# A recurrent attention block and a hashed mixture of experts in one kernel: which queue some loads stand on, where the inversion's steps stand on VectorE, and routing products cut into quarters

## The chip, the cores and the metric

The kernel runs on one core of a Trainium2 chip. The metric is the device time of one execution in microseconds (us); lower is better. Engines are called as in the profile: PE is TensorE's matmuls, PEld its weight loads, DVE is VectorE, ACT is ScalarE, POOL is GpSimd, SP is SyncE. A "q" behind an engine (SPq, POOLq) means the queue on which that engine issues DMAs.

## The reference, cut to what matters

```python
# attention: B, H, S, D = 4, 8, 768, 40, float32; state is D x D for each (batch, head)
for t in range(S):
    y[:, :, t] = einsum('bhd,bhde->bhe', r[t], state)
    Sa = einsum('bhde,bhe->bhd', state, a[t])
    state = state * w[t] - outer(Sa, b[t]) + outer(v[t], k[t])
x = y.transpose(0, 2, 1, 3).reshape(B * S, H * D)          # 3072 x 320
# experts: 8 of them, w1 320 x 1024, w2 1024 x 320
expert = token_ids * 2654435761 % 8
for e in range(8):
    out[expert == e] = relu(x[expert == e] @ w1[e]) @ w2[e]
```

## The kernel before

**Attention.** The sequence is cut into chunks of 64 steps. A tile is one chunk of two batches with all heads; there are 24 tiles, `u` = 0 to 23. Inside a chunk the recurrence becomes a triangular system: the products of the chunk's vectors are formed on PE (`z_ps`, `t_ps`, `a_ps`), the triangular matrix is inverted, and the state is carried from tile to tile by a chain of small products. The inversion (`group_i`) is done on DVE for four tiles at a time: one transposition (`nb`, L585), then 31 steps of two instructions each (`outer`, L595, and `ub`, L598), then transpositions out (`ut`, L603, and `um`, L609). The rest of a tile's chain is in `tile_m` and `tile_b`: `x_ps` and `u_ps` apply the inverse, `c_ps`, `rc_ps`, `nc_ps`, `s_ps`, `sd_ps`, `r_ps` and `y_ps` follow. DVE masks `rc_ps` into `mr` (L743), updates the state `sc` (L770) and forms `xs`, the product of y's PSUM tile with the decay `py` (L787), which POOL or SP stores to `x_rows` in DRAM. `decays` prepares the cumulative decays of `w` for each round of four tiles, on POOL and DVE.

**Order by ticks.** Nothing in this part is ordered by a scheduler. Each piece is registered with `at_tick(tick, ...)`, all pieces are sorted by tick, and every engine runs its instructions strictly in that order. Tile `u` runs its chain in tick `u + 8`; the 15 steps of a chain (`STEPS`) stand at fifteenths of a tick, so `rcv`, with DVE's `mr`, is at 4/15, `a` at 7/15 and `y` at 13/15. Group `gi` of the inversion starts at tick 4·gi + 3.5. Equal ticks are ordered by `order`, then by registration.

**PSUM.** `psum(...)` hands out two double-bank tiles in turn (`psa`), `bank(...)` two single banks in turn (`psb`). A product in a tile waits until what was two requests earlier in that ring has been read out. `x_ps` of a tile with `ti` not 0 stands at tick 0.1, right behind `y_ps` and `u_ps`, and takes the bank of `y_ps`, which `xs` reads.

**Routing** (`routing`, a generator whose pieces are advanced at the ticks of `when`) loads the token ids (`tok`), forms a one-hot `mine`, its sums by PE (`sums_ps`), ranks and slots on DVE, and in the end `slots_ps`: 24 products of a one-hot 128x128 (`at_pos`) with 53 columns (`tiles_f`), four at a time in six places between tiles 19 and 21. Its result gives the row indices of gather and scatter.

**Loads.** `first_weights` loads the first expert's weights in 12 DMAs, at ticks 20.5 to 27.1; each is `paced`, that is, it waits for the PE instruction that stands last before it. SP's queue also carries the tiles' inputs.

**Experts.** Behind the ticks a scheduler orders each engine's instructions at compile time, by program order and its own estimates; at run time each engine runs in the order fixed then. For each expert: `gather` (POOL, indirect DMAs), transposition on PE, `xt`; `up` (L1035, L1039; relu into `ht` on DVE for odd `f` and on ACT for even `f`, L1042 and L1044); `down` (L1059); a scatter (POOL, L1049). Expert 1's weights wait for expert 0's last gather; later ones for free buffers. Beside it the kernel reads all of `w` again, in 24 loads of 160 KB (`look`, tile `wt`, four buffers), and DVE checks that no value had to be clamped (`judge`, L1086 and L1087); only if one had does a slow loop run at the end. The first 16 of these loads stand on POOL's queue, the last 8 on SP's.

Of the kernel before, what the change touches and what calls it, by code (L numbers as in the profile page):

```python
# [8 lines left out]
F32 = mybir.dt.float32  # L9
I32 = mybir.dt.int32  # L10
AF = mybir.ActivationFunctionType
OP = mybir.AluOpType
# [6 lines left out]
def kernel(  # L19
# [13 lines left out]
    nc = tc.nc  # L33
    B, H, S, D = r.shape
    N, DM = out.shape
    E, _, F = moe_w1.shape
    assert (B * S, H * D) == (N, DM)
    P = 128
    C = 64
# [3 lines left out]
    NU = NCH * NG  # L43
    BLK = 32
    GRP = 4
    TPP = N // P
# [9 lines left out]
    NT = NST + NOV  # L56
    STEP = 8

    def pool(name, bufs, **kw):
        return ctx.enter_context(tc.tile_pool(name=name, bufs=bufs, **kw))  # L60

    const = pool("const", 1)
    route = pool("route", 1)
# [47 lines left out]
    def apool(name, bufs, **kw):  # L111
        return a_ctx.enter_context(tc.tile_pool(name=name, bufs=bufs, **kw))
# [7 lines left out]
    def turn_of(i):  # L120
        taken[i] += 1
        return taken[i] % 2
    psu = apool("psu", 1, space=bass.MemoryType.PSUM)

    R = 2 * C
    LAG = 8
# [23 lines left out]
    def at_tick(tick, step=None, order=0):  # L150
        if step is not None:
            tick += STEPS.index(step) / len(STEPS)

        def add(f):
            plan.append((round(tick, 4), order, len(plan), f))
            return f
        return add
# [52 lines left out]
    def psum(name):  # L210
        return psa.tile([P, 2, 512], F32, tag=f"psa{turn_of(0)}", name=name)

    def bank(shape, name):
        n = 1
        for s in shape[1:]:
            n *= s
        t = psb.tile([P, 512], F32, tag=f"psb{turn_of(1)}", name=name)[:, 0:n]
        return t if len(shape) == 2 else t.rearrange("p (x y) -> p x y", x=shape[1])

    def half(i):  # L220
        return slice(i * C, (i + 1) * C)
# [4 lines left out]
    def quarters():  # L226

        for hp in range(HP):
            for p in range(2):
                for be in range(2):  # L230
                    yield hp, p, be
# [3 lines left out]
    def mm(out_, lhsT, rhs, start=True, stop=True):  # L235
        pe_last[0] = nc.tensor.matmul(out_, lhsT=lhsT, rhs=rhs, start=start, stop=stop, skip_group_check=True).ins  # L236
# [383 lines left out]
    def tile_m(u, t0):  # L620

        x = tiles[u]
        gi, ti = divmod(u, GRP)

        t_x = t0 - 1.9 if ti else t0 - 1.4

        @at_tick(t_x)
        def _():
            ut = groups[gi]["ut"]
            x["x_ps"] = p = bank([P, H, BLK], "x_ps")  # L630
            for hp, par, be in quarters():
                h = hx(par, hp)
                top, low = slice(be * C, be * C + BLK), slice(be * C + BLK, (be + 1) * C)
                mm(p[low, h, :], x["no"][top, par, hp, BLK:], ut[top, ti * H + h, :])

        @at_tick(t_x + 0.115 if ti else t_x)
        def _():
            p = x.pop("x_ps")
            x["xi"] = xi = xi_r(u)
            for be in range(2):  # L640
                low = slice(be * C + BLK, (be + 1) * C)
                nc.scalar.copy(xi[low], p[low])

        @at_tick(*((t0 - 0.62,) if u and ti == 0 else (t0 - 1, "u")))
        def _():
            um, xi = groups[gi]["um"], x["xi"]
            x["um"] = um[:, ti * H:(ti + 1) * H, :]
            p = bank([P, H, BLK], "u_ps")
            for hp, par, be in quarters():
                h = hx(par, hp)  # L650
                top, low = slice(be * C, be * C + BLK), slice(be * C + BLK, (be + 1) * C)
                mm(p[top, h, :], xi[low, h, :], um[low, ti * H + h, BLK:])
            for be in range(2):
                top = slice(be * C, be * C + BLK)
                nc.scalar.copy(um[top, ti * H:(ti + 1) * H, BLK:], p[top])
# [147 lines left out]
    t_a = STEPS.index("a") / len(STEPS)  # L803
    decays(0, -9.0, -8.0, (-7.9, -7.6), -7.7, -7.5, -7.49, -7.48, None, -6.9, -7.2, -7.1)
    decays(1, -8.5, -7.09, (-7.08, -7.0), 0.85, 1.01, 1.02, 1.2, 1.03, 3.6, 1.05, (2.85, 2.0))
    decays(2, -5.5, 3.45, (5.61, 5.9), 6.2, 6.555, 6.56, 6.57, 6.561, 8.22, 6.58, (7.62, 7.55))
    for ri in range(3, NR):
        t = ri * RN * NG
        decays(ri, t - 5.8, *((7.75, (8.3, 8.9), 8.95) if ri == 3 else (t - 5.2, (t - 5.1, t - 3.9), t - 3.55)), t - 2.6, t - 2.59, t - 2.5, t - 2.45, t - 1.88, t - 2.4, (t - 0.9, t - 1.48))
# [5 lines left out]
    for gi in range(NU // GRP):  # L815
        t0 = gi * GRP + GRP - 1 + t_a
        if gi == 0:
            group_i(gi, 3.43, 3.47, 6.4, 6.401)
        else:
            group_i(gi, t0 + 0.03, t0 + 0.06, t0 + 2.68, gi * GRP + LAG - 0.99)  # L820


    ovin = route.tile([P, E], F32)
# [5 lines left out]
    def routing():  # L829
# [27 lines left out]
                                     op0=OP.mult, op1=OP.add)  # L857
# [56 lines left out]
        tiles_f = work.tile([P, (HC + 1) * D], F32, tag="qb", name="tiles_f", bufs=1)[:, 0:TPP * NT].rearrange("p (c n) -> p c n", n=NT)  # L914
# [5 lines left out]
        for i in range(3):  # L920
            shape, tag = ([P, BLK, BLK], "nb") if i == 1 else ([P, BH * D], "pt")
            at = work.tile(shape, F32, tag=tag, name="at_pos", bufs=1)[:]
            at = (at.rearrange("p a b -> p (a b)") if i == 1 else at[:, 0:per * P]).rearrange("p (c n) -> p c n", n=P)
            nc.vector.tensor_tensor(at, col[:].unsqueeze(1).to_broadcast([P, per, P]),
                                    place[:, 1, i * per:(i + 1) * per].unsqueeze(2).to_broadcast([P, per, P]), op=OP.is_equal)
            yield
            if i == 0:
                full_ps = psu.tile([P, BLK, BLK], F32, tag="ub", name="slots_ps")[:].rearrange("p s t -> p (s t)")[:, 0:NT]
            for c in range(per):
                k = i * per + c  # L930
                mm(full_ps, at[:, c], tiles_f[:, k], start=k == 0, stop=k == TPP - 1)
                if c % 4 == 3:
                    yield
        full = route.tile([P, NT], I32)
        nc.vector.tensor_scalar(full[:], full_ps, float(N), None, op0=OP.add)
        nc.vector.tensor_copy(idx_all[:, 0:NMT], full[:, 0:NMT])
        nc.sync.dma_start(slot_dram[:].rearrange("(p c) -> p c", p=P), full[:])
        for q in range(4):
# [18 lines left out]


    steps = routing()
    when = [22.25 + 0.1 * i for i in range(10)] + [24.4, 26.55, 26.9, 27.35, 27.75, 27.9, 28.35, 28.75, 28.9, 29.35, 29.75, 29.9, 29.95, 30.5]  # L960
    for t in when:
        at_tick(t, order=7)(lambda: next(steps, None))

# [2 lines left out]
    def first_weights():  # L966
        w1, w2 = moe_w1[0], moe_w2[0]
        h = HC * D
        a = [carry.tile([P, h], F32, tag="pb", name=f"w1_0{i}") for i in range(2)]
        b = carry.tile([P, 2, h], F32, tag="qt", name="w2_0", bufs=1)  # L970

        def hi(f):
            return a[f // 4][(f % 2) * C:(f % 2 + 1) * C, F + (f // 2 % 2) * P:F + (f // 2 % 2 + 1) * P]
        first_w[1] = lambda f, c: a[c][:, f * P:(f + 1) * P] if c < 2 else hi(f)
        first_w[2] = lambda f: b[:, f // 4, (f % 4) * DM:(f % 4 + 1) * DM]
        for i in range(2):
            for j in range(2):
                cols = slice(j * F // 2, (j + 1) * F // 2)
                yield nc.sync.dma_start(a[i][:, cols], w1[i * P:(i + 1) * P, cols])
            for x in range(2):  # L980
                yield nc.sync.dma_start(a[i][x * C:(x + 1) * C, F:].rearrange("p (f i) -> p f i", i=P),
                                        w1[2 * P:DM].rearrange("p (f x i) -> p x f i", x=2, i=P)[:, x, 2 * i:2 * i + 2])
        for i in range(2):
            for j in range(2):
                c0 = 4 * i + 2 * j
                yield nc.sync.dma_start(b[:, i, 2 * j * DM:2 * (j + 1) * DM].rearrange("p (c d) -> p c d", d=DM),
                                        w2[c0 * P:(c0 + 2) * P].rearrange("(c p) d -> p c d", p=P))

    weights = first_weights()
# [82 lines left out]
    wq = w.rearrange("b h (q t) e -> (b h q) (t e)", q=P // BH)  # L1072
    m = S * D * BH // (P * WP)
    seen = []

    def look(n):
        for i in range(len(seen), len(seen) + n):
            wt = mwork.tile([P, m], F32, tag="wt", name="wt", bufs=n)
            (nc.gpsimd if i < 16 else nc.sync).dma_start(wt[:], wq[:, i * m:(i + 1) * m])  # L1079
            seen.append(wt)  # L1080

    def judge(n):
# [61 lines left out]
    sel = seq.tile([P, B * H], F32, name="selq")  # L1144
# [5 lines left out]
    full = [P, DQ, D]  # L1150

    some = nc.values_load(ctl_i[0:1, 3:4], min_val=0, max_val=1)  # L1152
    with tc.For_i(0, some, 1):
        nblk = nc.values_load(ctl_i[0:1, 0:1], min_val=0, max_val=S // STEP)
        with tc.For_i(0, nblk, 1) as i:
            tsl = bass.ds(i * STEP, STEP)
            vec = {}
            for nm, src in (("w", w), ("a", a), ("b", b), ("k", k)):
                t = vec[nm] = seq.tile([P, STEP, D], F32, tag=f"in_{nm}", name=f"in_{nm}")
# [3 lines left out]
            for nm, src in (("v", v), ("r", r)):  # L1163
                t = vec[nm] = seq.tile([P, STEP, DQ], F32, tag=f"in_{nm}", name=f"in_{nm}")
# [34 lines left out]
        start = nc.values_load(ctl_i[0:1, 1:2], min_val=0, max_val=NST)  # L1199
        end = nc.values_load(ctl_i[0:1, 2:3], min_val=NST, max_val=NT)  # L1200
        with tc.For_i(start, end, 1) as i:
# [9 lines left out]
            w1 = load_w1(moe_w1[bass.ds(ereg, 1)].rearrange("one d f -> (one d) f"), "w1_ov")  # L1211
# [38 lines left out]
```

## Time and profile before

| | us |
|---|---|
| median of 3 runs (lowest to highest) | 698.65 (697.24 to 699.78) |
| the profiled execution | 697.15 |
| its span, first to last instruction | 695.4 |

| stretch of the span, us | PE busy | DVE busy | granted PE clock |
|---|---|---|---|
| 0 to 95 (loads, decays, first inversions) | 44.69 | 78.94 | 0.80 |
| 95 to 150 | 50.32 | 44.45 | 0.93 |
| 150 to 209 | 56.20 | 43.84 | 0.96 |
| 209 to 268 | 56.12 | 43.24 | 0.96 |
| 268 to 330 (routing begins) | 55.12 | 43.21 | 0.97 |
| 330 to 380 | 46.40 | 32.79 | 0.94 |
| 380 to 418 (last tiles) | 33.48 | 10.97 | 1.00 |
| 418 to 460 (experts begin) | 25.61 | 17.62 | 0.72 |
| 460 to 695 (experts) | 223.86 | 36.88 | 0.99 |

A row of a timeline is: start in us, duration in us, engine, line, operation, tile written and tiles read, shape, and xN for N instructions drawn together; in brackets stands how long the engine was idle just before and whose result ended the wait. PE's float32 product is recorded as two matmuls, so "x32" is 16 products. A granted clock of 1.00 is TensorE's upper level (2.4 GHz), 0.50 its lower one (1.2 GHz).

### The profile page before, as it was taken

Reading aid. Unit: us, or ns where it says so; the run is one execution under the profiler, and the core shown is the slowest. Engines: PE = TensorE matmul, PEld = TensorE weight load, DVE = VectorE, ACT = ScalarE, POOL = GpSimd, SP = SyncE. Lnnn points to the kernel's source line nnn. Section 1 sums busy time; section 2 is a strip of 40 time slices with the busy share of each in tenths; the row PEclk is TensorE's granted clock in tenths of the full one; section 3 lists DMA queues with packets and bytes.
Section 4 is the critical chain, followed back from the end, with each engine's and each line's share of the span. In section 5 each row is a group of like instructions: output and inputs, shape, how many; then the busy total and the mean of one; then the engine's idle time right before and its main releaser. Section 6 shows DMA issues by size and latency. Waiting matters only on the chain. (4 is left out here: it accounts for less than half of the span.)

```text
span 695.4 us, 23888 instructions
## 1 busy us (share of the span) xinstructions
PE 591.8 (85%) x10418; PEld 439.5 (63%) x10418; DVE 351.9 (51%) x747; ACT 263.8 (38%) x524; POOL 260.3 (37%) x352
## 2 busy tenths in 40 slices
PE   0356679989989999978899984699999999999995
PEld 0245668878878887867788872265655556565654
DVE  6969898677677857756873223335111111111110
ACT  1568547656666675646345320111011111111110
POOL 4439579785575733521131016312203030210101
PEclk9978569999999999999899995799999999999998
DMA  9875056655655455722333215992322442120000
GB/s 137 150 115 122 3 116 131 145 114 118 130 117 126 101 112 113 158 54 62 83 90 84 51 43 172 328 330 77 111 83 69 152 143 86 47 94 19 29 4 30
DMA packets 158125, 73.83 MB, mean 106 GB/s; under 512 B 132222, under 2 KB 151231, under 8 KB 158016
## 3 DMA queue, kind: packets, MB, share of 16 engines
q1 hardware_dynamic: 147840, 52.92, 34.3%
q0 software_dynamic: 5824, 18.36, 8.9%
q10 hardware_dynamic: 4352, 0.98, 1.2%
q8 instruction: 83, 1.36, 0.8%
q14 instruction: 26, 0.21, 0.1%
HBM read 56.71 MB, written 12.15 MB: 99 GB/s over the span
## 5 line engine op out<-in xcount | busy, mean ns | idle before, releaser
L1059 PE MATMUL dn_ps<-w,ht 128*128 128x320 f32 x384 | 105.1, 433 | 0.0
L1039 PE MATMUL up_ps<-xt,w 128*128 128x416 f32 x256 | 94.9, 524 | 0.0
L1059 PEld LDWEIGHTS dn_ps<-w,ht 128*128 128x128 f32 x384 | 72.7, 190 | 32.4 <-issue 2.4
L1049 POOL DMA_INDIRECT out_dram<-o,idx_all x26 | 26.1, 1002 | 171.4 <-ACT o L1048 167.3
L1039 PEld LDWEIGHTS up_ps<-xt,w 128*128 128x128 f32 x256 | 48.0, 193 | 47.0 <-issue 46.4
L790 POOL DMA_DIRECT2D x_rows<-xs x44 | 24.4, 558 | 127.6 <-DVE xs L787 59.6
L598 DVE TENSOR_TENSOR ub<-ub,outer 128x31 f32<-128x31 f32 (+15 forms) x186 | 65.0, 349 | 6.4
L595 DVE TENSOR_TENSOR outer<-ub,nb 128x31 f32<-128x31 f32 (+15 forms) x186 | 62.9, 338 | 6.2 <-ACT ub L578 1.2
L1042 DVE TENSOR_SCALAR ht<-up_ps 128x416 f32<-128x416 f32 x32 | 18.8, 591 | 84.5 <-PE up_ps L1039 84.5
L1025 DVE COPY xt<-xg_ps 128x384 f32<-128x384 f32 x24 | 12.1, 551 | 85.9 <-PE xg_ps L1024 85.9
L1048 ACT COPY o<-dn_ps 128x320 f32<-128x320 f32 x24 | 10.2, 426 | 101.8 <-PE dn_ps L1059 101.8
L557 PE MATMUL z_ps<-ident,z_all 128*128 128x128 f32 x192 | 31.6, 316 | 20.1 <-DVE z_all L494 9.7
L1035 PE MATMUL up_ps<-xt,w 64*128 64x416 f32 x128 | 30.2, 575 | 13.0 <-DVE ht L1042 6.2
L1044 ACT ACTIVATE ht<-up_ps 128x416 f32<-128x416 f32 x32 | 15.9, 515 | 66.7 <-PE up_ps L1039 66.7
L691 ACT COPY rv<-t_ps 128x1024 f32<-128x1024 f32 x24 | 24.3, 1012 | 42.1 <-PE t_ps L562 42.1
L557 PEld LDWEIGHTS z_ps<-ident,z_all 128*128 128x128 f32 x192 | 24.8, 162 | 23.7 <-POOL z_all L494 10.2
L1019 POOL DMA_INDIRECT xg<-x_rows,src_all x26 | 26.0, 999 | 33.3 <-PE xg_ps L1024 19.1
L754 ACT COPY x_all<-nc_ps 64x512 f32<-64x512 f32 x44 | 25.6, 581 | 30.2 <-PE nc_ps L752 29.9
L743 DVE TENSOR_TENSOR mr<-rc_ps,after 128x1024 f32<-128x1024 f32 x24 | 29.2, 1215 | 12.1 <-PE rc_ps L236 12.1
L494 POOL TENSOR_TENSOR z_all<-z_all,qt 128x320 f32<-128x320 f32 x40 | 33.8, 863 | 3.9 <-DMA z_all<-in_k_dram 3.9
L236 PEld LDWEIGHTS s_ps<-x_all,z_all 128*64 128x64 f32 x704 | 24.8, 146 | 11.5 <-issue 10.3
L1021 ACT COPY xg<-xg 128x64 f32<-128x64 f32 x26 | 6.4, 244 | 64.0 <-DMA xg<-x_rows,src_all 51.8
(194 smaller groups left out, 1169.2 us busy)
## 6 DMA issues: line engine op xcount, KB each, us to landing
w<-in_moe_w_dram SPq DMA_DIRECT2D x7, 1280.0 KB, 14.0
w<-in_moe_w_dram SPq DMA_DIRECT2D x7, 1024.0 KB, 5.4
r<-in_r_dram SPq DMA_DIRECT2D x48, 80.0 KB, 3.2
x_all<-in_v_dram SPq DMA_DIRECT2D x48, 80.0 KB, 2.8
py<-p_rows POOLq DMA_DIRECT2D x24, 160.0 KB, 3.2
z_all<-in_b_dram SPq DMA_DIRECT2D x46, 80.0 KB, 3.3
z_all<-in_k_dram SPq DMA_DIRECT2D x46, 80.0 KB, 3.6
qt<-qt SPq DMA_DIRECT2D x45, 80.0 KB, 2.9
```

Source lines behind the costliest of these rows:

```text
L236: pe_last[0] = nc.tensor.matmul(out_, lhsT=lhsT, rhs=rhs, start=start, stop=stop, skip_group_check=True).ins
L494: eng.tensor_tensor(t, t, by.rearrange("p (h e) -> p h e", e=D), op=OP.mult)
L557: pe_last[0] = nc.tensor.transpose(dst, src, ident[:]).ins
L595: nc.vector.tensor_tensor(tv, ub[:, 0:j + 1, j:j + 1].to_broadcast([P, j + 1, m]), nb[:, j, j + 1:].unsqueeze(1).to_broadcast([P, j + 1, m ...
L598: nc.vector.tensor_tensor(o, o, tv, op=OP.add)
L743: nc.vector.tensor_tensor(t[:].rearrange("p two h t -> p (two h) t"), p[:].rearrange("p two (h t) -> p (two h) t", t=C), after[:].unsqueez ...
L754: nc.scalar.copy(x["x"][half(be), be], p[half(be)])
L1019: g = nc.gpsimd.indirect_dma_start(out=xg[:, 0:DM], out_offset=None, in_=x_rows[:], in_offset=bass.IndirectOffsetOnAxis(ap=idx, axis=0))
L1035: nc.tensor.matmul(banks[-1][:], lhsT=w1(f, 2), rhs=xt[part(f), 2, 0:n], start=True, stop=False)
L1039: nc.tensor.matmul(p[:], lhsT=w1(f, c), rhs=xt[:, c, 0:n], start=False, stop=(c == 1))
L1049: st = nc.gpsimd.indirect_dma_start(out=out[:], out_offset=bass.IndirectOffsetOnAxis(ap=idx, axis=0), in_=o[:], in_offset=None, bounds_che ...
L1059: nc.tensor.matmul(p[:], lhsT=ht[:, f, j * P:(j + 1) * P], rhs=w2(f), start=(f == 0), stop=(f == FP - 1))
```

## The change

- `x_ps` of tiles 18, 19, 21, 22 and 23 (`u >= NU - LAG + 2` and `ti`) takes a tile of the `psa` ring in place of a bank of the `psb` ring.
- The second-round `decays` turn their end values (`en_ps`) at tick 9.45 in place of 8.22.
- For groups 1 to 5 the 31 inversion steps start 0.27 in place of 0.06 of a tick behind `t0`, and the transposition `ut` stands at 2.75 in place of 2.68; the steps are spread evenly by cost between the two.
- Each one-hot product of `slots_ps` is cut into four 64x64 quarters that accumulate in two banks; DVE adds the two halves (one more instruction).
- Routing's second piece (`sums_ps`) moves from tick 22.35 to 22.85, the eight DVE pieces behind it from 22.45 to 23.15 to 22.95 to 23.37.
- The 12 loads of the first expert's weights move from SP's queue to POOL's.
- The first 16 of the 24 loads of `w` for the check move from POOL's queue to SP's.

```diff
@@ tile_m
-            x["x_ps"] = p = bank([P, H, BLK], "x_ps")
+            if u >= NU - LAG + 2 and ti:
+                p = psum("x_ps")[:, 0, 0:H * BLK].rearrange("p (h t) -> p h t", h=H)
+            else:
+                p = bank([P, H, BLK], "x_ps")
+            x["x_ps"] = p
@@ calls of decays and group_i
-    decays(2, -5.5, 3.45, (5.61, 5.9), 6.2, 6.555, 6.56, 6.57, 6.561, 8.22, 6.58, (7.62, 7.55))
+    decays(2, -5.5, 3.45, (5.61, 5.9), 6.2, 6.555, 6.56, 6.57, 6.561, 9.45, 6.58, (7.62, 7.55))
-            group_i(gi, t0 + 0.03, t0 + 0.06, t0 + 2.68, gi * GRP + LAG - 0.99)
+            group_i(gi, t0 + 0.03, t0 + 0.27, t0 + 2.75, gi * GRP + LAG - 0.99)
@@ routing
-                full_ps = psu.tile([P, BLK, BLK], F32, tag="ub", name="slots_ps")[:].rearrange("p s t -> p (s t)")[:, 0:NT]
+                full_ps = psu.tile([P, BLK, BLK], F32, tag="ub", name="slots_ps")[:].rearrange("p s t -> p (s t)").rearrange("p (two x) -> p two x", two=2)[:, :, 0:NT]
-                mm(full_ps, at[:, c], tiles_f[:, k], start=k == 0, stop=k == TPP - 1)
+                for i_, j in ((0, 0), (1, 1), (0, 1), (1, 0)):
+                    mm(full_ps[half(j), i_], at[half(i_), c, half(j)], tiles_f[half(i_), k], start=k == 0, stop=k == TPP - 1)
-        nc.vector.tensor_scalar(full[:], full_ps, float(N), None, op0=OP.add)
+        part = route.tile([P, NT], F32, name="part", tag="sel")
+        nc.vector.tensor_scalar(part[:], full_ps[:, 0], float(N), None, op0=OP.add)
+        nc.vector.tensor_tensor(full[:], part[:], full_ps[:, 1], op=OP.add)
-    when = [22.25 + 0.1 * i for i in range(10)] + [24.4, 26.55, 26.9, 27.35, 27.75, 27.9, 28.35, 28.75, 28.9, 29.35, 29.75, 29.9, 29.95, 30.5]
+    when = [22.25, 22.85] + [22.95 + 0.06 * i for i in range(8)] + [24.4, 26.55, 26.9, 27.35, 27.75, 27.9, 28.35, 28.75, 28.9, 29.35, 29.75, 29.9, 29.95, 30.5]
@@ first_weights (the other two loads there likewise)
-                yield nc.sync.dma_start(a[i][:, cols], w1[i * P:(i + 1) * P, cols])
+                yield nc.gpsimd.dma_start(a[i][:, cols], w1[i * P:(i + 1) * P, cols])
@@ look
-            (nc.gpsimd if i < 16 else nc.sync).dma_start(wt[:], wq[:, i * m:(i + 1) * m])
+            nc.sync.dma_start(wt[:], wq[:, i * m:(i + 1) * m])
```

## Rows read from the trace of the kernel before

**Rows 1.** Waits, 95 to 345 us: total us, times, longest

```profile
PE x_ps L236 <- DVE xs L787: 7.5, 4, 2.3
```

**Rows 2.** Timeline of PE, a tile with a wait and one without

```profile
147.05 0.69 PE L236 MATMUL x_ps<-ut,nk 32*32 32x32 f32 x32 [1.75 <-DVE xs L787]
147.68 0.69 PE L236 MATMUL rc_ps<-rv,cv 64*64 64x64 f32 x32
...
152.07 0.76 PE L236 MATMUL s_ps<-sc,ident 64*64 64x320 f32 x4
...
162.29 0.69 PE L236 MATMUL rc_ps<-rv,cv 64*64 64x64 f32 x32
...
165.59 0.76 PE L236 MATMUL s_ps<-sc,ident 64*64 64x320 f32 x4
```

**Rows 3.** Timeline of DVE at the same wait, 143 to 147 us

```profile
144.62 0.28 DVE L595 TENSOR_TENSOR outer<-ub,nb 128x112 f32<-128x112 f32 x1
...
146.52 0.48 DVE L787 TENSOR_TENSOR xs<-y_ps,py 128x320 f32<-128x320 f32 x1
```

**Rows 4.** Stretches: length, busy us of PE, PEld, DVE, ACT, POOL; granted clock; DMA

```profile
149.00:151.00 2.00, 2.00 (x37) 1.78 (x37) 1.72 (x4) 1.75 (x4) 1.94 (x3) 0.50 0.79 137
303.80:309.10 5.30, 5.30 (x145) 4.72 (x138) 4.65 (x19) 4.26 (x8) 0.00 (x0) 1.00 0.11 19
```

**Rows 5.** Timeline of PE from 327 to 346 us

```profile
327.48 0.69 PE L236 MATMUL x_ps<-ut,nk 32*32 32x32 f32 x32 [2.32 <-DVE xs L787]
...
331.40 1.33 PE L236 MATMUL s_ps<-sc,ident 64*64 64x320 f32 x4 [1.06 <-ACT xi L642]
...
345.51 0.76 PE L236 MATMUL s_ps<-sc,ident 64*64 64x320 f32 x4 [1.39 <-ACT xi L642]
```

**Rows 6.** Timeline of PE in tile 0

```profile
97.25 1.97 PE L557 MATMUL t_ps<-ident,at 128*128 128x128 f32 x8 [1.77 <-DVE mr L743]
```

**Rows 7.** Timeline of PE and DVE where routing begins, ticks 22 and 23

```profile
298.72 0.93 PE L846 MATMUL sums_ps<-mine,ones 128*128 128x192 f32 x2 [3.14 <-DVE mine L840]
...
300.22 1.33 PE L236 MATMUL s_ps<-sc,ident 64*64 64x320 f32 x4
...
302.87 1.16 PE L236 MATMUL a_ps<-at_t,z_t 64*64 64x64 f32 x64
...
317.64 1.16 PE L236 MATMUL a_ps<-at_t,z_t 64*64 64x64 f32 x64
...
298.49 1.22 DVE L743 TENSOR_TENSOR mr<-rc_ps,after 128x1024 f32<-128x1024 f32 x1
...
314.40 1.22 DVE L743 TENSOR_TENSOR mr<-rc_ps,after 128x1024 f32<-128x1024 f32 x1
```

**Rows 8.** Timeline of PE, four of the 24 one-hot products

```profile
380.48 1.10 PE L236 MATMUL slots_ps<-tiles_f,at_pos 128*128 128x53 f32 x8
```

**Rows 9.** Timeline of PE, first and second expert

```profile
431.08 3.14 PE L1035 MATMUL up_ps<-xt,w 64*128 64x416 f32 x8 [1.66 <-DVE xt L1120]
...
449.24 1.76 PE L1035 MATMUL up_ps<-xt,w 64*128 64x416 f32 x4 [6.19 <-DVE ht L1042]
...
457.32 13.31 PE L1059 MATMUL dn_ps<-w,ht 128*128 128x320 f32 x48
...
472.54 1.67 PE L1035 MATMUL up_ps<-xt,w 64*128 64x416 f32 x8 [0.85 <-DVE xt L1025]
...
487.20 13.08 PE L1059 MATMUL dn_ps<-w,ht 128*128 128x320 f32 x48
```

**Rows 10.** Timeline of DVE in the first expert

```profile
448.35 0.33 DVE L1086 TENSOR_SCALAR wc<-wt 128x320 f32<-128x320 f32 x1 [3.70 <-DMA wt<-in_w_dram]
448.60 0.58 DVE L1042 TENSOR_SCALAR ht<-up_ps 128x416 f32<-128x416 f32 x1
```

**Rows 11.** DMA issues of the check's loads: count, KB each, median us to landing

```profile
wt<-in_w_dram POOLq DMA_DIRECT2D x16, 160.0 KB, 5.9
...
wt<-in_w_dram SPq DMA_DIRECT2D x8, 160.0 KB, 8.1
```

More of the change, by code (lines that the diff above doesn't have):

```diff
@@ L978, in first_weights @@
                 cols = slice(j * F // 2, (j + 1) * F // 2)
-                yield nc.sync.dma_start(a[i][:, cols], w1[i * P:(i + 1) * P, cols])
+                yield nc.gpsimd.dma_start(a[i][:, cols], w1[i * P:(i + 1) * P, cols])
             for x in range(2):
-                yield nc.sync.dma_start(a[i][x * C:(x + 1) * C, F:].rearrange("p (f i) -> p f i", i=P),
+                yield nc.gpsimd.dma_start(a[i][x * C:(x + 1) * C, F:].rearrange("p (f i) -> p f i", i=P),
                                         w1[2 * P:DM].rearrange("p (f x i) -> p x f i", x=2, i=P)[:, x, 2 * i:2 * i + 2])
@@ L985, in first_weights @@
                 c0 = 4 * i + 2 * j
-                yield nc.sync.dma_start(b[:, i, 2 * j * DM:2 * (j + 1) * DM].rearrange("p (c d) -> p c d", d=DM),
+                yield nc.gpsimd.dma_start(b[:, i, 2 * j * DM:2 * (j + 1) * DM].rearrange("p (c d) -> p c d", d=DM),
                                         w2[c0 * P:(c0 + 2) * P].rearrange("(c p) d -> p c d", p=P))
```

## The prediction

> **What bounds the kernel now.** I read the stretches first (the table above): from 95 us on PE is busy nearly all the time, so the end is set by PE's own work and by the places where PE waits. The list of waits then names them, the timelines show what stands in front of each, and a stretch gives the clock behind it. What the reader is to see are five places.
>
> *x_ps behind xs.* PE waits four times for `xs`, 7.5 us in all [rows 1]; they are tiles 3, 7, 11 and 15, the ones in which an inversion begins. `x_ps` needs the bank that `xs` reads, and `xs` stands on DVE behind six inversion steps of two instructions [rows 3]. The wait of 1.75 us [rows 2] is followed by a stretch at a granted clock of 0.50, TensorE's lower level [rows 4]: from `rc_ps` to `s_ps` PE needs 152.07 - 147.68 = 4.39 us there and 165.59 - 162.29 = 3.30 us in tile 4, which had no such wait [rows 2]. So each wait costs its own length and about 1.1 us of slower products.
>
> *s_ps behind xi.* In the late tiles, which have no more input products to fill the time, `s_ps` waits for ACT to empty the bank of `x_ps` (`xi`): 1.06 and 1.39 us [rows 5].
>
> *The start.* In tile 0 PE waits 1.77 us for `mr`, which stands on DVE behind inversion steps [rows 6].
>
> *Routing's sums.* PE stops 3.14 us at `sums_ps` because `mine` waits for the token ids to land [rows 7].
>
> *The first expert.* `up` of expert 0 takes 457.32 - 431.08 = 26.24 us, that of expert 1 only 487.20 - 472.54 = 14.66 [rows 9]. Most of the 11.6 us between them is one wait of 6.19 us for the relu `ht` on DVE [rows 9], and `ht` was late because the check's `wc` stood in front of it, waiting for a load of `w` [rows 10].
>
> **The change part by part.** The sum starts from the profiled execution, 697.15 us.
>
> *Inversion steps later.* With the steps spread by their costs over 2.48 in place of 2.62 ticks, those that fall before 13/15 of the first tick go from six to three. `xs` then starts where the fourth step stood, 144.62, in place of 146.52: 1.90 us earlier, more than the wait of 1.75 [rows 2, 3]. Tiles 3, 7 and 11 share 7.5 - 2.32 = 5.2 us [rows 1, 5] and get back 3 x 1.1 of clock: **-8.5**. Bounds: 0, if DVE then sets the pace; -8.5 at most. The three steps are not gone; they land between `xs` and the next `mr`. After them `mr` would start about when `rc_ps` ends, and `mr` has slack: what waits for it first is `a_ps`, which in tile 15 began 317.64 - 315.62 = 2.0 us after its end [rows 7]. I take the full gain.
>
> *x_ps in the other ring.* For tile 18 this removes the fourth wait behind `xs` altogether (2.32 us) and the wait behind `xi` that followed (1.06); for tile 19 it removes 1.39 [rows 5]. With 1.1 of clock for the first: **-5.9**. Tiles 21 to 23 give less each and are left as margin. What replaces the wait: in the `psa` ring `x_ps` waits for ACT's read of the `rv` products, made before `u_ps` ends, so it comes a tenth late at worst. Bounds: -3.3 (the clock not returned, tile 19's wait half) to -7.
>
> *The start.* The steps start 0.21 of a tick later in group 1 as well, so the decay transpositions of round 2 go ahead of them and `mr` of tile 0 comes sooner; moving `en_ps` out of the same tick takes away a product that queued for a bank. I take the wait of `t_ps`, **-1.8** [rows 6]; bounds 0 and -2.5 (with the lower clock's share). `en_ps` at its new place is one product, and its result is wanted six tiles later.
>
> *Routing's pieces.* `sums_ps` no longer stops PE, but DVE still waits for the token ids in front of `mr`. `mr` ends at 298.49 + 1.22 = 299.71, and `a_ps` needs the tile that it reads; so `a_ps` can start at 299.7 in place of 302.87, 3.2 us earlier, while the sums' own 300.22 - 298.72 = 1.5 us are spent later in the tick: 1.7 gained [rows 7]. Against it, DVE pieces of 5.3 us (303.80 to 309.10, DVE busy 4.65 [rows 4]) move from an idle place in tick 22 to the stretch between `xs` and `mr` of tick 23. `mr` there is late by up to 5.3 us, and `a_ps` has 2.0 of slack [rows 7]: a new wait of 0 to 3.3, the middle being 1.7. Net **0**, bounds -1.7 and +1.6.
>
> *Quarters.* Four whole one-hot products take 1.10 us (x8 records) [rows 8]; sixteen 64x64 quarters of 64 columns, the `rc_ps` products, take 0.69 (x32) [rows 2]. The quarters here have 53 columns and go to four corners in turn as those do. Six places of 0.41: **-2.5**; bounds 0 and -2.5. The added DVE instruction is of the size of an inversion step's half, 0.28 us [rows 3], and delays one `mr` by it: **+0.3**.
> The Trainium skill (TensorEngine Tiling, Instruction Overhead) says that every matmul carries about 60 cycles of overhead, so that one with a free dimension of 1 takes as long as one of 60, and warns against cutting a dimension that is small already. By that, four times as many matmuls of 53 columns gain nothing, and the sum ends 2.5 us higher. The two rows above say otherwise for this kernel's own shapes, so I keep them.
>
> *The first expert's weights on POOL.* Twelve issues leave SP and go to POOL. SP is not waited for here. On POOL each waits for PE's last instruction as it did on SP; behind it stand the stores of `xs`, the loads of `py` and POOL's masks and multiplications, whose results are wanted most of a tick later. The weights are used from 431 us on [rows 9], more than three ticks after the last of the twelve: **0**. If that cover were gone, `up` would start late by the landing of one load, 5.9 us [rows 11].
>
> *The check's loads on SP.* On POOL these sixteen stood between gathers and raced the next experts' weights. On SP the first of them can go out while SP waits for expert 0's last gather (its weights are held until then), so DVE can judge them in the time in which it waits for gathers; the others line up with the weights, and the relu no longer waits, if the scheduler puts the checks where SP delivers them. What can be gained is 6.19 (the wait), up to 1.66 at the start of `up` (`xt` behind a `wc`), and part of the slower clock: 11.6 + 1.7 = 13.2 at most, since `up` of expert 1 shows the time without [rows 9]. At least 0, or a loss (rivals). I take **-8**, the two waits, because expert 0 will still begin at the lower clock.
>
> Sum: -8.5 - 5.9 - 1.8 + 0 - 2.5 + 0.3 + 0 - 8 = -26.4, so 670.8 for an execution like the profiled one. The median of the runs stands 1.5 above that execution; I forecast **672 us**.
>
> **The rivals.**
> *The relu still waits (680 us).* The check's loads on SP took 8.1 us to land, longer than POOL's 5.9 [rows 11]. If they land as late as now and stand in front of the relu as now, the 8 us stay: 672 + 8 = 680. For it: the DMAs still carry the same bytes. Against it: SP's order lets the first loads out before the weights.
> The Trainium skill (DMA: Bandwidth & Descriptors, Issuing engines are not separate DMA queues) says the same as a rule: DMAs issued from any engine run on the same 16 DMA engines and interleave, and another queue saves only the issue time. By it the last part is worth nothing. The rows of landing times do differ by queue, but they come from different moments.
>
> *DVE becomes the pace of the tiles (681 us).* If the inversion can't follow a faster PE, the 8.5 of the first part come back as waits for `mr` or `ut`. Against it: in the table by stretches DVE is busy 43 to 44 of 59 us where inversions run.
>
> *Slower: SP's order puts check loads behind the weights (over 699 us).* Place: `up` of expert 0. If the checks stay in front of the relus in DVE's order, but their loads stand on SP behind megabytes of weights, every round of four checks costs a landing of 8.1 us [rows 11], and four buffers allow no more than one round at a time. Without the last part the sum is -18.4. The present excess of `up` is 11.6, so four such rounds (32.4) cost 20.8 more than now: 697.15 - 18.4 + 20.8 = 699.6, 701 against the median. Three rounds cost 12.7 more and still end faster, at 693. From the fourth round in front of a relu the change is slower. For it: a scheduler that misjudged POOL's landing can misjudge SP's. Against it: the last eight checks are on SP already, and their rounds made no relu of expert 1 late enough to stop PE (14.66).
>
> *Quarters gain nothing (674.5 us).* If a product's fixed cost counts and not its size, sixteen small ones for four large ones cost at least as much as before, and 2.5 us come back. For it: the quarters are no shorter in columns. Against it: rows 2 and 8, shape for shape.
>
> *Little change.* The waits of `x_ps` and of the relu are in the rows with what ended them; that all of them stay is unlikely.
>
> **How the numbers follow.** Forecast, relu free and tiles faster: 0.57, 664 to 677. Relu still waits: 0.20, 678 to 685. DVE paces: 0.10, 676 to 685. SP rounds: two or three 0.07 (685 to 695), four or more 0.05 (over 699). Quarters without gain add 2.5 to any of these, 1 in 10. Little change: 0.01. The lower end takes the favourable bounds: -7 for the ring, -2.5 at the start, -1.7 for routing, -11 for the expert: 672 - 1.1 - 0.7 - 1.7 - 3 = 665.5, and some 3 less for tiles 21 to 23 and the longer wait's clock in tile 15: 662. The upper end holds the second and third cases with their bounds: 688. A measurement of this kernel can tell a difference from about 0.3% (2 us): faster by more 0.93 (three rounds still end at 695), within it 0.02, slower 0.05.
>
> **What the profile after would show.** Right: no wait of `x_ps` for `xs` but for fractions; the granted clock near 1.00 behind those tiles; `s_ps` of tiles 16 and 17's ticks (24 and 25) without a wait for `xi`; `slots_ps` groups of 32 records in about 0.7 us; `a_ps` in place of `sums_ps` as the wait of tick 22; `up` of expert 0 in 17 to 19 us. Wrong: a wait of `a_ps` or `x_ps` for `mr` or `ut` in the inversion's ticks; `wc` in front of `ht` with a wait for `wt` of 8 us or more; gathers landing later because loads of `w` go out beside them.

## The result, and the profile after

The changed kernel takes 676.97 us (median of 4 runs, 673.82 to 677.77), the kernel before 699.21 us (4 runs) beside it: a ratio of 0.967, 95% interval 0.963 to 0.972. The profiled execution took 677.77 us; its span is 675.9 us after 695.4, so 19.5 us less. The forecast was 672, with 26.4 us less. Two of the kernels further down (the token ids' load alone and the quarters alone) had one and two executions in a slower state, at a lower granted clock: they are in the median and the range, and not in the ratio.

Where the 19.5 us came from can be read off the starts of `rc_ps<-rv,cv` on PE, one in each tile, and of `up` and `dn` (a "tile" here lasts from its `rc_ps` to the next one's, so that `x_ps` of a later tile stands in it):

| stretch | before | after | difference |
|---|---|---|---|
| start, and tiles 0 to 2 | 131.50 | 130.19 | -1.31 |
| tiles 3, 4, 7, 8, 11, 12 | 92.33 | 83.56 | -8.77 |
| tiles 5, 6, 9, 10 | 55.31 | 55.46 | +0.15 |
| tile 13 | 13.51 | 14.77 | +1.26 |
| tile 14 (token ids) | 19.30 | 19.54 | +0.24 |
| tiles 15 to 17 | 42.15 | 36.28 | -5.87 |
| tile 18 | 11.07 | 16.43 | **+5.36** |
| tiles 19 to 22 (`slots_ps`) | 47.90 | 43.88 | -4.02 |
| last `rc_ps` to `up` of expert 0 | 18.01 | 17.79 | -0.22 |
| `up` of expert 0 | 26.24 | 16.85 | -9.39 |
| from its end to `up` of expert 1 | 15.22 | 17.02 | **+1.80** |
| `up` of expert 1 | 14.66 | 16.32 | **+1.66** |
| the rest | 208.20 | 207.81 | -0.39 |

The list of PE's waits from 95 to 345 us after the change (total us, times, longest) answers [rows 1]: no wait of `x_ps` for `xs` is left. In tick 22 `a_ps` waits for `mr` where `sums_ps` waited before, and in tick 23 it waits again.

```profile
PE a_ps L236 <- DVE mr L747: 3.4, 1, 3.4
...
PE s_ps L236 <- ACT xi L646: 1.5, 4, 0.4
PE a_ps L236 <- DVE ovtok L900: 1.1, 1, 1.1
```

On DVE `xs` of tile 3 stands behind three inversion steps, which were six in [rows 3]; this is the third of them and `xs`:

```profile
143.01 0.26 DVE L598 TENSOR_TENSOR ub<-ub,outer 128x87 f32<-128x87 f32 x1
143.19 0.49 DVE L791 TENSOR_TENSOR xs<-y_ps,py 128x320 f32<-128x320 f32 x1
```

The granted clock between 150 and 268 us is 1.00 after 0.96. The stretch of tile 18 shows the opposite (columns as in [rows 4]):

```profile
150.00:209.00 59.00, 56.74 (x1661) 48.35 (x1653) 46.31 (x94) 39.30 (x75) 39.66 (x56) 1.00 0.60 124
209.00:268.00 59.00, 57.47 (x1719) 49.53 (x1721) 45.82 (x94) 39.00 (x75) 28.74 (x33) 1.00 0.58 119
...
347.00:354.00 7.00, 6.66 (x107) 6.34 (x108) 2.15 (x4) 0.55 (x2) 2.31 (x1) 0.52 0.07 21
```

PE's timeline there shows what went ahead of the lower clock:

```profile
339.80 0.69 PE L236 MATMUL rc_ps<-rv,cv 64*64 64x64 f32 x32 [0.40 <-ACT cv L730]
...
345.65 0.69 PE L236 MATMUL x_ps<-ut,nk 32*32 32x32 f32 x32 [0.72 <-DVE ut L603]
347.34 1.33 PE L236 MATMUL r_ps<-sc,at_t 128*64 128x80 f32 x16 [1.00 <-DVE sc L774]
348.60 1.93 PE L236 MATMUL r_ps<-x_all,nk 64*64 64x40 f32 x32
```

and DVE's timeline why: the last group's `ut` begins late, and `mr` and the state `sc` stand behind it.

```profile
343.54 1.96 DVE L603 STREAM_TRANSPOSE ut<-ub 128x1024 f32<-128x1024 f32 x1
345.36 1.20 DVE L747 TENSOR_TENSOR mr<-rc_ps,after 128x1024 f32<-128x1024 f32 x1
346.48 0.81 DVE L774 TENSOR_TENSOR sc<-s_ps,pend 128x640 f32<-128x640 f32 x1
```

This `ut` starts 3.74 us behind `rc_ps` of tile 18 (339.80). Before the change it started 0.27 us behind it (354.10):

```profile
354.37 1.95 DVE L603 STREAM_TRANSPOSE ut<-ub 128x1024 f32<-128x1024 f32 x1
```

In the experts (PE's timeline, answering [rows 9]) the wait of `up` for `ht` is gone, but expert 1 now waits 2.88 us for `xt`, and its `up` runs at a granted clock of 0.90, after 1.00 before:

```profile
417.90 3.14 PE L1042 MATMUL up_ps<-xt,w 64*128 64x416 f32 x8 [1.19 <-DVE xt L1127]
...
434.75 13.08 PE L1066 MATMUL dn_ps<-w,ht 128*128 128x320 f32 x48
451.77 1.83 PE L1042 MATMUL up_ps<-xt,w 64*128 64x416 f32 x8 [2.88 <-DVE xt L1032]
```

On DVE it is again a round of `wc` in front, now of `xt`; [rows 10] showed it in front of `ht`. The first row below tells what freed the relu: the loads of `w` are still late, but the round that waits for them stands behind expert 0's last `ht` (434.95) in DVE's order.

```profile
441.63 0.33 DVE L1093 TENSOR_SCALAR wc<-wt 128x320 f32<-128x320 f32 x1 [6.09 <-DMA wt<-in_w_dram]
...
446.77 0.33 DVE L1093 TENSOR_SCALAR wc<-wt 128x320 f32<-128x320 f32 x1 [2.48 <-DMA wt<-in_w_dram]
...
450.24 1.48 DVE L1032 COPY xt<-xg_ps 128x384 f32<-128x384 f32 x3
```

### The profile page after: what moved, and what is told of

It reads as the page before. It is cut to its first block, busy times and chain, and to the rows that moved or that the text cites. A ratio compares the mean times of both kernels' runs of the same rounds, so it can differ in the third digit from the quotient of the medians.

```text
span 675.9 us, 24173 instructions
## 1 busy us (share of the span) xinstructions
PE 583.2 (86%) x10562; PEld 434.8 (64%) x10562; DVE 350.4 (52%) x748; ACT 264.4 (39%) x524; POOL 258.3 (38%) x348
## 4 chain that ended last, share of the span: by engine, by line
PE 35%; issue 34%; DVE 11%; DMA 6%; POOL 6%; ACT 4%; SPq 2%; POOLq 0%; DVEq 0%; ACTq 0%
PE r_ps L236 6%; PE y_ps L236 5%; PE s_ps L236 4%; POOL out_dram L1056 3%; PE sd_ps L557 3%; PE a_ps L236 3%; PE rc_ps L236 3%; POOL xg L1026 3%; DVE ub L598 3%; DVE outer L595 3%; PE t_ps L562 2%; PE t_ps L557 2%; PE nc_ps L756 1%; DMA z_all<-in_k_dram 1%; PE u_ps L236 1%
## 5 line engine op out<-in xcount | busy, mean ns | idle before, releaser
L1055 ACT COPY o<-dn_ps 128x320 f32<-128x320 f32 x24 | 10.2, 426 | 101.6 <-PE dn_ps L1066 101.6
L1042 PE MATMUL up_ps<-xt,w 64*128 64x416 f32 x128 | 28.3, 563 | 7.7 <-DVE xt L1032 5.3
L538 ACT COPY nk<-a_ps 128x1024 f32<-128x1024 f32 x21 | 21.3, 1013 | 25.9 <-PE a_ps L236 25.7
```

The source lines that it names most:

```text
L1042: nc.tensor.matmul(banks[-1][:], lhsT=w1(f, 2), rhs=xt[part(f), 2, 0:n], start=True, stop=False)
```

## The experiments

All stretches below are read as in the table above, each from one profiled execution. Where an edit does not touch them, the stretch to tile 3 varies by 1.8 us (130.1 to 131.9 in the kernels made from the one before) and tile 14 from 19.3 to 21.0. Medians of before are those of the same session (698.49, 699.54 and 699.57 us).

| kernel | to `rc_ps` of tile 3 | tiles 3, 4, 7, 8, 11, 12 | 14 | 15 to 17 | 18 | 19 to 22 |
|---|---|---|---|---|---|---|
| before | 131.50 | 92.33 | 19.30 | 42.15 | 11.07 | 47.90 |
| changed | 130.19 | 83.56 | 19.54 | 36.28 | 16.43 | 43.88 |
| before + steps | 128.03 | 85.49 | 20.42 | 37.92 | 11.54 | 47.99 |
| before + ring | 130.33 | 92.63 | 20.97 | 37.29 | 11.75 | 46.95 |
| before + quarters | 131.76 | 92.64 | 20.74 | 41.05 | 11.07 | 46.29 |
| changed, group 5 at old ticks | 129.76 | 84.23 | 21.01 | 37.97 | 11.75 | 44.96 |
| changed, token ids' load early | 129.42 | 84.36 | 17.05 | 36.27 | 16.92 | 46.60 |
| changed, three edits | 130.24 | 83.63 | 19.21 | 37.30 | 11.78 | 45.09 |
| changed, `eid` in a pause of POOL | 129.94 | 84.76 | 14.54 | 36.28 | 13.47 | 44.38 |
| changed, five edits | 130.14 | 83.46 | 14.36 | 36.44 | 12.58 | 43.71 |

### The inversion's steps alone

```diff
-            group_i(gi, t0 + 0.03, t0 + 0.06, t0 + 2.68, gi * GRP + LAG - 0.99)
+            group_i(gi, t0 + 0.03, t0 + 0.27, t0 + 2.75, gi * GRP + LAG - 0.99)
```

> The kernel before with one part alone: the inversion's steps of groups 1 to 5 start at 0.27 and end at 2.75 ticks behind t0. Theory (each step moved out from in front of xs removes a wait of x_ps and its slow clock, and only the last group's ut comes too late): tiles 3, 7, 11 and 15 give back 2.6 + 3.4 + 2.7 (the growth of the lead in the trace of the changed kernel) and some 3 more, and the last group takes back up to 5, since the ticks behind it are short: net about -7 us. Rival (DVE is the pace of the tiles): what goes in front of xs comes back as waits for mr or ut in every group, and the time stays within 2 us of before.

Measured: 684.34 us, ratio 0.978 (0.974 to 0.982); the last `mr` starts 13.2 us earlier than before, as much as in the whole changed kernel (13.0). The gain lies in the six tiles (-6.84), in tiles 15 to 17 (-4.23, for tile 15 is a tile with an inversion's start too) and at the beginning (-3.47). Twice as much as expected, since the last group cost nothing here: its `ut` started 1.94 us behind `rc_ps` of tile 18 and PE did not wait for it, for PE itself still waited 1.39 us for `xi` twice and was less far ahead of DVE. That DVE sets the pace of every group is refuted.

### The other ring alone

The first hunk of the change, applied to the kernel before.

> The kernel before with one part alone: x_ps of tiles 18, 19, 21, 22 and 23 in the other PSUM ring. Theory of the prediction: the fourth wait behind xs (2.3 us), the two waits behind xi (1.1 and 1.4 us) and the lower clock (1.1 us) go: -5.9 us. Rival: the new ring has its own waits (for the copies of rv and cv on ACT, or for mr) and only the first wait goes: -2 to -3 us.

Measured: 694.23 us, ratio 0.992 (0.990 to 0.995), so about 5 us less: tiles 15 to 17 give 4.86, tiles 19 to 22 another 0.95. The size of the term is as forecast. But beside the steps it is worth less: they take the wait in tile 15 already, and from the steps alone (37.92) to the changed kernel (36.28) tiles 15 to 17 give only 1.64 more.

### Group 5 back at its old ticks

```diff
-            group_i(gi, t0 + 0.03, t0 + 0.27, t0 + 2.75, gi * GRP + LAG - 0.99)
+            group_i(gi, t0 + 0.03, t0 + (0.27 if gi < 5 else 0.06), t0 + (2.75 if gi < 5 else 2.68), gi * GRP + LAG - 0.99)
```

> The changed kernel with group 5's inversion back at its old ticks (0.06 and 2.68). Theory (the steps of the last group, now half a step of their old lead later against shorter ticks, make x_ps of tile 20 wait for ut, then r_ps for the state, and the clock falls): 16.4 us between rc_ps of tiles 18 and 19 go back to about 11, so -5 us against the changed kernel, some 672. Rival (x_ps in the other ring or the routing's pieces make that loss): the time stays within 1 us of the changed kernel, or the wait of x_ps for xs comes back.

Measured: 676.93 us, as the changed kernel. Tile 18 falls from 16.43 to 11.75: the late `ut` made that loss. Tiles 15 to 17 take back 1.69 (more steps stand in front of `xs` and `sc`; `y_ps` waits 0.73 and 0.49 us for `sc`), tiles 19 to 22 1.08, and tile 14, which the edit does not touch, was 1.47 longer. The cause is shown; going back is no remedy.

### Quarters alone

The hunk of `slots_ps` and the two DVE lines, applied to the kernel before.

> The kernel before with one part alone: slots_ps in quarters, with the one more DVE instruction. Theory of the prediction: six groups of 32 records in about 0.7 us in place of 8 in 1.10, -2.2 us in all. Rival (a fixed cost for each product): groups of 1.1 us or more, 0 to +1 us. Second rival (something else sets the pace of those tiles): groups of 0.7 us, and the last mr no earlier.

Measured: 698.0 us, ratio 0.998 (0.995 to 1.000), too small a difference for the times. The products of the changed kernel, by form (ns, least, median, most of one):

```profile
L236 PE MATMUL slots_ps<-tiles_f,at_pos x192: 209/218/258, 358.0 to 386.7; 64*64 64x53 f32 x192
```

A group of 32 records that stands by itself in the timeline takes 0.64 to 0.73 us (8 took 1.10), here as in the changed kernel; the first group here has a pause in it and lasts 1.15. Tiles 19 to 22 become 1.6 us shorter, of some 2 that the groups save. By the rule weighed in the prediction (the Trainium skill, TensorEngine Tiling (Array Packing), Instruction Overhead) nothing would have been gained; the rows say otherwise for these shapes.

### The two queue changes, apart and together

Four kernels, all from the one before. The loads of `w` alone:

```diff
-            (nc.gpsimd if i < 16 else nc.sync).dma_start(wt[:], wq[:, i * m:(i + 1) * m])
+            nc.sync.dma_start(wt[:], wq[:, i * m:(i + 1) * m])
```

> The kernel before with one part alone: the first 16 loads of w for the check on SP's queue; the first expert's weights stay on SP. Theory (the queue alone frees the relus, and the new wait of expert 1's xt behind the checks takes some back): the first up in about 17 us in place of 26.2, the start of the second up 3 to 4 us later behind dn, -6 to -7 us in all. Rival (the first expert's weights have to leave SP too, or the loads come late): less than 3 us gained.

Measured: 700.28 us, ratio 1.005 (1.001 to 1.008): nothing gained, and a little lost. Yet `up` of expert 0 took 16.94 us and `up` of expert 1 began at 464.58 in place of 472.54. The gain is lost behind all work: POOL's last scatter ends at 683.04, and the span at 697.7 (POOL's timeline, and the line of the core):

```profile
682.06 0.98 POOL L1049 DMA_INDIRECT out_dram<-o,idx_all  x1 [3.32 <-ACT o L1048]
```
```profile
core 0: 697.7 us, clock 0.931
```

Before, it is 690.19 and 695.4:

```profile
689.20 0.98 POOL L1049 DMA_INDIRECT out_dram<-o,idx_all  x1 [3.32 <-ACT o L1048]
```

Among the instructions that the views leave out, the trace holds a DRAIN on POOL behind that last scatter: 9.88 us here, 1.30 before and 0.97 in the changed kernel. Then both queue changes together (the weights' three `dma_start` to `nc.gpsimd` as well), the weights alone, and the loads of `w` with only the four loads of the second matrix on POOL:

> The kernel before with both queue changes and nothing else: the first expert's weights on POOL, the first 16 loads of w on SP. With the loads of w alone (the run before this one) the second up began 8.0 us earlier, and the end came 14.7 us behind POOL's last scatter in place of 5.2. Theory (the long end comes with the number of DMAs that POOL issues, 120 there, 136 before, 132 in the changed kernel): here with 132 the end is 5 us again and the kernel is 6 to 7 us faster than before. Rival (the long end comes from the loads of w on SP): it stays, and the time is that of before within 2 us.

> The kernel before with the first expert's weights on POOL alone, so 148 DMAs from POOL. Theory of the prediction (the weights' queue is worth nothing by itself): the relu waits 6.2 us as before, the time is that of before within 2 us, and the end behind the last scatter stays near 5 us. Rival (the weights' queue is what frees the relus or the tiles): 5 us or more gained. If the end behind the last scatter follows POOL's number of DMAs in another way, it shows here.

> The kernel before with all loads of w on SP and 4 of the 12 loads of the first expert's weights (those of its second matrix) on POOL: 124 DMAs from POOL. Theory (POOL's last drain takes 82 ns for each DMA since about the 120th, as 0.97 us at 132, 1.30 at 136 and 2.28 at 148 fit, and 9.9 us when only 120 were issued): a drain of about 0.3 us, the end 4 to 5 us behind the last scatter, 8 to 10 us faster than the run with 120. Rival (the long end belongs to the loads of w on SP, or all twelve weights have to move): the end stays 14 us behind the last scatter, and the time within 2 us of that run.

| kernel | DMAs from POOL | DRAIN, us | end behind last scatter, us | median, us (before) |
|---|---|---|---|---|
| loads of `w` on SP | 120 | 9.88 | 14.7 | 700.28 (698.49) |
| and 4 loads of weights on POOL | 124 | 10.20 | 15.1 | 700.20 (699.57) |
| and all 12 on POOL | 132 | 0.97 | 4.7 | 691.60 (699.54) |
| before | 136 | 1.30 | 5.2 | 698.65 |
| weights alone on POOL | 148 | 2.28 | 6.6 | 702.42 (699.54) |

Together the two are worth 8 us (ratio 0.988, 0.984 to 0.992), each alone is a small loss. The drain goes with the count: in all seven kernels here with 132 DMAs it took 0.97 us, in all four with 136 it took 1.30, whatever else was changed. My theory of a threshold at about 120 fell: with 124 DMAs the drain grew to 10.2. What fits the five counts is 0.08 us for each DMA that POOL has issued, with some 120 of them struck off at a point between 125 and 132 DMAs. What strikes them off is not settled, and no run counts through that gap.

### The token ids

One tick earlier, load alone (with a `yield` behind it, and 21.25 put in front of the ticks of `when`):

```diff
         nc.sync.dma_start(tok[:], tok_h.bitcast(I32).rearrange("(p c two) -> p c two", p=P, two=2))
+        yield
         token = const.tile([P, TPP], I32)
...
-    when = [22.25, 22.85] + ...
+    when = [21.25, 22.25, 22.85] + ...
```

> The changed kernel with the load of the token ids one tick earlier (21.25 in place of 22.25); the pieces behind it stay. Theory (mr of tick 22 stands on DVE behind the wait for the token ids; a_ps waits for mr 3.4 us and runs with its successors at a lower clock, some 1.5 us): -4 to -5 us against the changed kernel, no wait of a_ps for mr in tick 22. Rival (mr is late because of DVE's own work, or the DVE pieces of tick 23 take what is gained): less than 1.5 us.

Measured: 679.49 us (676.23 to 686.52), ratio 0.970 (0.966 to 0.974): no gain. Nothing waits for the load any more, but `mr` is only 1.0 us earlier behind its `rc_ps`, because `eid`, the first instruction that reads the ids, now takes 2.67 us itself. In the changed kernel it took 0.18, behind the wait for the load:

```profile
290.26 0.18 DVE L842 TENSOR_SCALAR eid<-tok 128x24 int32<-128x24 int32 x1 [3.31 <-DMA tok<-in_moe_token_ids_dram]
```

Tile 14 becomes 2.5 us shorter; tiles 19 to 22 were 2.7 us longer in this execution. DVE's timeline with the earlier load, then POOL's:

```profile
285.87 2.67 DVE L843 TENSOR_SCALAR eid<-tok 128x24 int32<-128x24 int32 x1
```
```profile
285.99 0.88 POOL L494 TENSOR_TENSOR at<-at,pt 128x320 f32<-128x320 f32 x1
286.82 1.68 POOL L494 TENSOR_TENSOR z_all<-z_all,qt 128x320 f32<-128x320 f32 x2
```

`eid` ends at 288.54, POOL's last product at 288.50. So the wait for the load had covered another, for POOL: this is argued from the two ends here, and tested by the next kernel. Then `eid` and `mine` in a pause of POOL (ticks 20.5 for the load, 21.7 for the two):

> The changed kernel with the token ids' load at 20.5 and eid and mine at 21.7; sums_ps and the pieces behind it stay. With the load alone a tick earlier, eid no longer waited but took 2.67 us in place of 0.18, and ended when POOL's products of z_all ended. Theory (eid and POOL's products can't run side by side): in a pause of POOL eid takes 0.2 us again, mr of tick 22 starts when rc_ps ends, a_ps waits for nothing: 3 us and up to 1.5 us of clock of that tick go. The whole gains less, as the late ut takes back up to 3 us. Rival (eid is slow by itself when it doesn't wait): 2.6 us again at the new place, on DVE in the inversion's steps.

Measured: 672.30 us (668.07 to 675.52), ratio 0.963 (0.960 to 0.967). `eid` takes 0.17 us in the pause, `mr` follows `rc_ps`, and `a_ps` waits for nothing:

```profile
279.09 0.17 DVE L843 TENSOR_SCALAR eid<-tok 128x24 int32<-128x24 int32 x1
```
```profile
288.39 1.16 PE L236 MATMUL a_ps<-at_t,z_t 64*64 64x64 f32 x64
289.48 1.09 PE L557 MATMUL sd_ps<-ident,sc 128*128 128x128 f32 x8
```

Tile 14 falls from 19.54 to 14.54. That `eid` is slow by itself is refuted: in twelve of the fourteen profiled kernels no product of POOL runs beside it and it takes 0.17 or 0.18 us; in the two others (2.67, and 2.62 in the next kernel) it ends with the third of three such products. By the Trainium skill (SBUF — State Buffer, SBUF: two separate sides) DVE and POOL share one pair of ports under an exclusive lock, and whichever starts later is blocked for the whole of the other's instruction; for DVE the page limits this to instructions in a two-port mode or with two inputs in SBUF. The rows agree that `eid` was held up, but through three products and not one, and no run shows which mode it ran in.

In tile 18 this kernel has the waits of the changed one to 0.01 us (0.72 for `ut`, 0.99 for `sc`), but the clock stayed at 1.00 from 342 to 348 us, and the tile took 13.47 in place of 16.43. So of the 5.36 us lost there, 2.96 are the lower clock.

```profile
340.42 0.69 PE L236 MATMUL x_ps<-ut,nk 32*32 32x32 f32 x32 [0.72 <-DVE ut L603]
342.11 0.78 PE L236 MATMUL r_ps<-sc,at_t 128*64 128x80 f32 x16 [0.99 <-DVE sc L774]
```
```profile
342.00:348.00 6.00, 5.36 (x176) 4.97 (x176) 3.83 (x5) 1.93 (x3) 3.92 (x4) 1.00 0.26 61
```

### Putting it together

Three edits on the changed kernel (load of the ids at 21.25, routing's other pieces at their ticks of before, group 5 from 0.27 to 2.5):

> The changed kernel with three edits: token ids one tick earlier, routing's pieces back at their ticks of before (sums_ps at 22.35 and so on), the last group's inversion from 0.27 to 2.5 in place of 2.75. Theory: the wait of a_ps in tick 22 (3.4 us and 1.5 us of clock) goes, that in tick 23 (1.1 us) goes since DVE's pieces stand in tick 22 again, and the late ut (0.7 and 1.0 us of waits and some 3 us of clock) goes: -8 to -10 us against the changed kernel, 667 to 669. Rival (each wait is followed by another resource just as late): less than 4 us.

Measured: 674.79 us, ratio 0.966 (0.963 to 0.970), so 2 us less than the changed kernel, as the rival had it. `eid` took 2.62 us here too and `sums_ps` waited 3.06. Tile 18 was healed (11.78), although the last group's steps still start at 0.27: what was too late is the group's end at 2.75, with `ut`, and not its start.

Five edits (listed in the expectation; the loads of the check in 20 pieces, each held until its expert's last gather):

```diff
-            group_i(gi, t0 + 0.03, t0 + 0.27, t0 + 2.75, gi * GRP + LAG - 0.99)
+            group_i(gi, t0 + 0.03, t0 + 0.27, t0 + (2.75 if gi < 5 else 2.6), gi * GRP + LAG - 0.99)
...
-    when = [22.25, 22.85] + [22.95 + 0.06 * i for i in range(8)] + ...
+    when = [20.5, 21.7] + [22.35 + 0.1 * i for i in range(9)] + ...
...
+        if 1 < e < E - 1:
+            held.append(g)
+            look(per)
+            held.pop()
```

> The changed kernel with five edits: the token ids' load at 20.5, eid and mine at 21.7 (POOL has a pause there), sums_ps and the DVE pieces from 22.35 to 23.15, the last group's inversion from 0.27 to 2.6, and the check in 20 loads of 192 KB that wait for the last gather of their expert (experts 2 to 6) in place of 24 loads at once. Theory: no wait for mine or mr in tick 22 (3.4 us and 1.5 us of clock), none for ut (1.7 us and 3 us of clock), none of the second up for xt behind the checks (2.9 us and 1.7 us of clock): -10 to -13 us against the changed kernel, 664 to 667. Rival (the other resource is just as late each time, as with the earlier token ids alone): 672 to 676.

Measured: 674.10 us (668.91 to 678.21), ratio 0.965 (0.961 to 0.969). The tiles came out nearly as expected: the last `mr` starts at 390.67, 10.7 us ahead of the changed kernel's 401.35. Expert 1's `xt` is no longer behind the check. But in the later experts the held loads arrive when the relus are due, and the old pattern is back, on PE and on DVE:

```profile
509.01 0.97 PE L1043 MATMUL up_ps<-xt,w 64*128 64x416 f32 x4 [1.71 <-DVE ht L1050]
```
```profile
506.50 0.36 DVE L1094 TENSOR_SCALAR wc<-wt 128x384 f32<-128x384 f32 x1 [7.60 <-DMA wt<-in_w_dram]
```

The lowest median is that of the kernel with `eid` in POOL's pause. The intervals of these kernels overlap with that of the changed kernel, so none is shown to beat it by its times; what is shown is tile 14. The five edits' tiles with the changed kernel's loads of the check were not run.

## Why the prediction was right, and where it was not

The direction and the two largest terms were right for the reasons given. The median lies at the very edge of the 664 to 677 us of that case, and as well in the 676 to 685 of the case that DVE paces the tiles; what tells the two apart are the rows, not the time. Several terms came near by other ways than they were argued.

*Inversion steps later (-8.5).* Right in mechanism, and in size for the tiles that it names: -8.77 in the six tiles (-6.84 with the steps alone), all in the pairs named, with the clock back at 1.00. Wrong was a step of its bounds: "The three steps are not gone; they land between `xs` and the next `mr`", from which only `mr` was followed up, and the move of `ut` from 2.68 to 2.75 got no price. The step "what waits for it first is `a_ps`" failed for the last group: what came late were `ut`, for which `x_ps` of tile 20 waits, and `sc`. With waits of 1.7 us and 3 us of lower clock tile 18 took back 5.36 us. The prediction had this as a rival for all groups (DVE paces the tiles); it holds for one, where the ticks are shortest. This is the largest part of the 6.9 us between the forecast's 26.4 and the 19.5 of the profiled executions.

*The other ring (-5.9).* Tiles 15 to 17 gave 5.87 in the changed kernel. The sum was right, its attribution less so: the steps alone take the wait of tile 15 as well, so that the two edits share some 3 us (4.23 + 4.86 - 5.87).

*The start (-1.8).* -1.31, within what this stretch varies. As forecast, `mr` of tile 0 starts sooner behind its `rc_ps`, 9.09 us after it in place of 11.43. But the wait that was priced has not gone: `t_ps` waits 1.82 us for `mr`, after 1.77 [rows 6], for inversion steps still stand in front of `mr` and PE gets there sooner too.

```profile
94.17 1.97 PE L557 MATMUL t_ps<-ident,at 128*128 128x128 f32 x8 [1.82 <-DVE mr L747]
```

What went in front of it is the wait of `en_ps` for `xi`, 2.01 us, of which `s_ps` has 0.95 now. Tile 0 became 1.64 us shorter, and tile 1 gave 1.04 of it back: it takes 13.52 to 13.53 us in the six profiled kernels with `en_ps` at 9.45, where `en_ps` waits 0.72 us for `sc` in front of `a_ps`, and 12.48 to 12.49 in the eight with the old place. The steps alone gave 3.47. The move was not run by itself. That the sum came near the length of a wait that stayed was luck.

*Routing's pieces (0).* +0.24 in tile 14; in tick 23 `a_ps` waits 1.12 us, by my reading for `mr` behind the pieces (forecast 1.7; the profile names `ovtok`, which DVE runs just behind `mr`). The forecast's `a_ps` did start 2.1 us earlier after its `rc_ps` (8.13 in place of 10.22), and gave 1.5 back at a lower clock.

*Quarters (-2.5, +0.3).* The groups are as forecast; the tiles show 1.6 alone, and 4.0 in the changed kernel. The ring alone gave 0.95 there, so 1.5 of the 4.0 show in no run of a single edit.

*First weights on POOL (0).* Failed: by itself it loses some 3 us (702.42 after 699.54), but without it the loads of `w` bring nothing, for the end behind the last scatter takes 14.7 us in place of 4.7. The next term was kept by luck, since the change happened to hold both. No view of before shows the drain, only the 5.2 us between the last scatter and the span's end.

*Loads of w on SP (-8).* -9.39 in `up` of expert 0, its 16.85 us just below the 17 to 19 forecast: the rival of a relu that still waits did not come. Overlooked was that the checks, moved out from in front of the relus, gather in front of the next expert's `xt`: +1.80 and +1.66. Net -5.9, and -6.5 for all behind the last `rc_ps`.

Tile 13 (+1.26) was in no term; 0.92 of it is a wait of `rc_ps` that the profile gives to nothing ("issue").

## What to carry over

When an engine is given slack by moving work behind a deadline, list everything that stands behind the moved work, not the first reader alone: here `mr` had slack, and `ut` and the state in the shortest ticks had none. Where two edits remove the same wait, count it once. Where two edits are one change, run each alone: here the queue of the first weights, priced at nothing, decided whether the other queue change paid. A wait's named releaser is only the last of several: before pricing its removal, look at what the other engines do until then.

## What was not expected of the hardware

- A DRAIN on POOL at the end takes 0.97, 1.30 and 2.28 us with 132, 136 and 148 DMAs issued from POOL, and 9.88 and 10.20 with 120 and 124.
- A DVE instruction of 128x24 took 2.67 and 2.62 us in place of 0.18 and ended with POOL's products; the trace shows no wait for it, only a longer instruction.
- The same two waits (0.72 and 0.99 or 1.00 us) were followed by a granted clock of 0.52 in one execution and 1.00 in another.
